# Three reorderings around tiles 3 to 8 of a fused linear-attention and SwiGLU kernel: one aggregation, two z sums, one clip and max-add

## The chip, the cores and the metric

The kernel runs on one core of a Trainium2 chip. The metric is the device time of one execution in microseconds (us). The engines are named as in the profile: PE is TensorE (PEld its weight loads), DVE is VectorE, ACT is ScalarE, POOL is GpSimd, SP is SyncE (SPq its queue of issued DMAs).

## What is computed

The input x has 2048 rows of 512 numbers. It is normalised row by row, and the result xn feeds a linear attention with 32 heads of 16 and a gated feed-forward block of width 1792. Both outputs are added to x.

```python
def _A_ref(x, wqkv, wo):                      # linear attention
    ...
    phi = lambda t: jnp.where(t > 0, t + 1, jnp.exp(t)) + 1e-6
    pq, pk = phi(q), phi(k)
    kv = jnp.einsum("bhsd,bhse->bhde", pk, v)
    z = jnp.einsum("bhsd->bhd", pk)
    num = jnp.einsum("bhqd,bhde->bhqe", pq, kv)
    den = jnp.einsum("bhqd,bhd->bhq", pq, z)[..., None] + 1e-6
    o = num / den
    return ... o ... @ wo

def _B_ref(x, w_gate, w_up, w_down):          # gated feed-forward
    return (_silu(x @ w_gate) * (x @ w_up)) @ w_down

xn = _layernorm(x, axis=-1)
return x + _A_ref(xn, A_wqkv, A_wo) + _B_ref(xn, B_w_gate, B_w_up, B_w_down)
```

## The kernel before

The 2048 rows are 16 tiles of 128 rows, and a tile is 128x512. The kernel has a front part, in which every tile is normalised, projected to keys and queries and accumulated, and a feed-forward part, in which TensorE runs the gate, up and down projections and the attention output for the rest of the span. The change touches the front part alone.

Every instruction is appended by hand to a list of its engine, in the order in which the calls stand in the program. An engine runs its list in order. `K.op` and `K.dma` take the names that an instruction reads (`r`) and writes (`w`), and put in front of it the semaphore waits that follow from earlier writers and readers. So the order of the calls sets the order on each engine, and a name in `r` that the instruction does not need for its data is a way to hold it back: it waits for the last writer of that name.

What happens to a tile t, with the lines at which its instructions appear in the profile:

- `bns(t)` (L297) and `agg(t)` (L300), on DVE: the row statistics, and mean and variance from them.
- `eps(t, "pool")` (L325) and `rstd_of(t)` (L334), on POOL: variance plus 1e-5, and its power of -0.5, both of one number per row. `stat(t)` is these four in a row.
- `xn(t)`: `xn_dve(t)` (L314), on DVE, normalises the tile, and `transpose_dma(t)` (L408), issued on SP, writes the transposed tile to `xnT`. Tile 3 is normalised by `xn_dve(3)` and transposed later.
- `kproj(t)` and `qproj(t)` (L417), on PE: four matmuls each, from `xnT` to a PSUM bank. Tiles 0 to 3 are projected before they are normalised (`proj_first`, L431) and scaled by `rstd` when the bank is read.
- `exp_k(t)` (L465), `exp_q(t)` (L471) and `copy_q(t)` (L477), on ACT: they read those banks. For the first tiles `first_ek` (L501) and `first_pk` (L507) do so, the latter into `kpos`.
- `clip_k(t)` (L484) and `maxadd_k(t)` (L493), on DVE: they turn the exponential and the bank into the key feature `pkq[:, t, 0, :]`. For tiles 1 to 3 `first_feat(t)` (L533) adds `kpos` and the clipped exponential instead, both in SBUF.
- `zsum(t, e)` (L557 for tile 0, L561 for the others), on POOL: adds the tile's key feature to `zacc`. Tile 0's is a cast, which starts the sum. The argument e names a buffer of exponentials whose last writer it waits for.
- `gtacc(t)` (L569), on PE: four matmuls that add the product of the normalised tile and its key feature to four PSUM banks. It needs `xn` and the key feature of the tile.

The order on PE around the change is `proj_first(3)`, `gtacc(1)`, `gtacc(2)`, `kproj(4)`, `qproj(4)`, `gtacc(3)`, `kproj(5)`, `qproj(5)`, `gtacc(4)`, `kproj(6)`, `qproj(6)`, `gtacc(5)` and so on. The order on POOL is `rstd(3)`, `rstd(5)`, `eps(6)`, `rstd(6)`, `zsum(0)`, `eps(7)`, `rstd(7)`, `eps(8)`, `rstd(8)`, `zsum(1)`, `eps(9)`, `rstd(9)`, `zsum(2)`. On DVE it is `xn(5)`, `bns(6)`, clip 3, `agg(6)`, `first_feat(3)`, `xn(6)`, `xn(3)`, `bns(7)`, `agg(7)`, `bns(8)`, `agg(8)`, clip 4, `xn(7)`, max-add 4, `bns(9)`, `agg(9)`, `xn(8)`, clip 5, max-add 5. SP issues the transpose of tile 6, the load of the input tiles 14 and 15, and the transposes of tiles 7, 8 and 9.

From tile 5 on a loop writes the steps of a tile: the two projections, the three ACT readings, the normalisations in `XN0[t]`, `feat_k(t)` (clip, then the z sum of tile t - 3, then max-add), and the statistics in `STAT[t]`.

Of the kernel before, what the change touches and what calls it, by code (L numbers as in the profile page):

```python
# [14 lines left out]
NT = S // P  # L15
# [93 lines left out]
def bass_parallel_sum__linear_attn_block__swiglu_ffn__prompt_kernel(  # L109
# [13 lines left out]
    pe, act, dve, pool, sp = nc.tensor, nc.scalar, nc.vector, nc.gpsimd, nc.sync  # L123
    bf, f32 = dt.bfloat16, dt.float32

    with contextlib.ExitStack() as es:
        E = es.enter_context

        def sb(name, shape, d=bf):
            return E(nc.sbuf_tensor(name, [P] + shape, d))  # L130
# [20 lines left out]
        NE = 3  # L151
        ek = sb("ek", [NE, D])
# [37 lines left out]
        def bk(i):  # L190
            return ("bank", i)
# [10 lines left out]
        def xload(eng, h, t0, n, after=()):  # L202
            K.dma(
                eng, lambda: h.dma_start(x_sb[:, t0:t0 + n, :], rows(xin, t0, n)),
                r=list(after), w=[("x", t0 + i) for i in range(n)],
            )
# [89 lines left out]
        def bns(t):  # L296
            K.op("dve", lambda: dve.bn_stats(stats[:, t, :], x_sb[:, t, :]), r=[("x", t)], w=[("st", t)])  # L297

        def agg(t):
            K.op("dve", lambda: dve.bn_aggr(mv[:, t, :], stats[:, t, :]), r=[("st", t)], w=[("mv", t)])  # L300
# [10 lines left out]
        def xn_dve(t):  # L311
            K.op(
                "dve",
                lambda: dve.tensor_scalar(  # L314
                    out=xn_sb[:, t, :], in0=x_sb[:, t, :], scalar1=mv[:, t, 0:1], scalar2=rstd[:, t:t + 1],
                    op0=ALU.subtract, op1=ALU.mult,
                ),
                r=[("x", t), ("mv", t), ("rstd", t)], w=[("xn", t)],
            )

        def eps(t, eng):
            h = dve if eng == "dve" else pool
            K.op(
                eng,
                lambda: h.tensor_scalar(  # L325
                    out=vpe[:, t:t + 1], in0=mv[:, t, 1:2], scalar1=1e-5, scalar2=None, op0=ALU.add,
                ),
                r=[("mv", t)], w=[("vpe", t)],
            )

        def rstd_of(t):
            K.op(
                "pool",
                lambda: pool.tensor_tensor(out=rstd[:, t:t + 1], in0=vpe[:, t:t + 1], in1=nhalf[:, :], op=ALU.pow),  # L334
                r=[("vpe", t), ("nhalf",)], w=[("rstd", t)],
            )
# [89 lines left out]
        def proj_first(t, wname, h):  # L426
            lo, b = (D, kb(t)) if wname == "wk" else (0, qb(t))
            K.op(
                "pe",
                [  # L430
                    (lambda c=c: pe.matmul(  # L431
                        banks[b], xcT[:, NDC * t + c, :], wqkv_sb[:, c, lo:lo + D],
                        start=(c == 0), stop=(c == NDC - 1),
                    ))
                    for c in (2 * h, 2 * h + 1)
                ],
                r=[("xcT", t, h)] + [(wname, i) for i in ((2, 3) if h else (0, 1))], w=[bk(b)],
            )
# [12 lines left out]
        def kb(t):  # L451
            return 2 * (t % 2)

        def qb(t):
            return 2 * (t % 2) + 1

        def kproj(t):
            proj(t, kb(t), D, "wk")

        def qproj(t):  # L460
            proj(t, qb(t), 0, "wq")
# [7 lines left out]
        def exp_q(t):  # L469
            K.op(  # L470
                "act", lambda: act.activation(eq[:, t, :], banks[qb(t)], ACT.Exp),  # L471
                r=[bk(qb(t))], w=[("eq", t)],
            )
# [16 lines left out]
        def maxadd(dst, src, e, r, w):  # L490
            K.op(
                "dve",
                lambda: dve.scalar_tensor_tensor(  # L493
                    out=dst, in0=src, scalar=0.0, in1=e, op0=ALU.max, op1=ALU.add,
                ),
                r=r, w=w,
            )
# [7 lines left out]
        def first_pk(t):  # L505
            K.op(
                "act", lambda: act.activation(kpos[:, t % NE, :], banks[kb(t)], ACT.Relu, scale=rstd[:, t:t + 1]),  # L507
                r=[bk(kb(t)), ("rstd", t)], w=[("kpos", t % NE)],
            )
# [7 lines left out]
        def first_pq(t):  # L517
            K.op(
                "act", lambda: act.activation(pkq[:, t, 1, :], banks[qb(t)], ACT.Identity, scale=rstd[:, t:t + 1]),
                r=[bk(qb(t)), ("rstd", t)], w=[("pq", t)],  # L520
            )
# [8 lines left out]
        def first_feat(t):  # L530
            K.op(
                "dve",
                lambda: dve.tensor_tensor(out=pkq[:, t, 0, :], in0=kpos[:, t % NE, :], in1=ek[:, t % NE, :], op=ALU.add),  # L533
                r=[("kpos", t % NE), ("ek", t % NE)], w=[("pk", t)],
            )

        def clip_k(t):
            clip(ek[:, t % NE, :], ("ek", t % NE))

        def maxadd_k(t):  # L540
            e = t % NE
            maxadd(pkq[:, t, 0, :], banks[kb(t)], ek[:, e, :], [bk(kb(t)), ("ek", e)], [("pk", t)])

        def feat_k(t):
            clip_k(t)
            zsum(t - 3, t % NE)
            maxadd_k(t)

        def feat_q(t):
            clip(eq[:, t, :], ("eq", t))  # L550
            maxadd(pkq[:, t, 1, :], pkq[:, t, 1, :], eq[:, t, :], [("eq", t), ("pq", t)], [("pq", t)])

        def zsum(t, e):
            pk = pkq[:, t, 0, :]
            after = [] if e is None else [("ek", e)]
            if t == 0:
                K.op("pool", lambda: pool.tensor_copy(zacc[:, :], pk), r=[("pk", t)] + after, w=[("zacc",)])  # L557
            else:
                K.op(
                    "pool",  # L560
                    lambda: pool.tensor_tensor(out=zacc[:, :], in0=zacc[:, :], in1=pk, op=ALU.add),  # L561
                    r=[("pk", t), ("zacc",)] + after, w=[("zacc",)],
                )

        def gtacc(t):
            K.op(
                "pe",
                [
                    (lambda c=c: pe.matmul(  # L569
                        banks[4 + c], xn_sb[:, t, c * P:(c + 1) * P], pkq[:, t, 0, :],  # L570
                        start=(t == 0), stop=(t == NT - 1),
                    ))
                    for c in range(NDC)
                ],
                r=[("xn", t), ("pk", t)], w=[bk(4 + c) for c in range(NDC)],
            )

        def stat(t):
            bns(t)
            agg(t)  # L580
            eps(t, "pool")
            rstd_of(t)

        def xn(t):
            xn_dve(t)
            if t >= 3:
                transpose_dma(t)
# [92 lines left out]
        rstd_of(5)  # L680
        xn(5)
        bns(6)
        first_pq(2)
        proj_first(3, "wk", 1)
        first_ek(3)
        clip_k(3)
        first_pk(3)
        agg(6)
        eps(6, "pool")
        rstd_of(6)  # L690
        zsum(0, 0)
        first_feat(3)
        gtacc(1)
        gtacc(2)
        xn(6)
        xload("sp", sp, 14, 2)
        xn_dve(3)
        bns(7)
        kproj(4)
        agg(7)  # L700
# [2 lines left out]
        exp_k(4)  # L703
        first_pq(3)
        qproj(4)
        stat(8)
        exp_q(4)
        copy_q(4)
        clip_k(4)
        zsum(1, 1)  # L710
        xn(7)
        maxadd_k(4)
        bns(9)
        agg(9)
        eps(9, "pool")
# [7 lines left out]
        for t in range(5, NT):  # L723
            kproj(t)
            exp_k(t)
            qproj(t)
            exp_q(t)
            copy_q(t)
            for i in XN0.get(t, ()):
                xn(i)  # L730
            feat_k(t)
            for i in STAT.get(t, ()):
                stat(i)
            for i in XN.get(t, ()):
                xn(i)
            if t in (6, 7, 8, 9):
                transpose_dma((3, 0, 1, 2)[t - 6])
            if t == 10:
                whalf("wg", wg_sb, B_w_gate, 0)
                whalf("wu", wu_sb, B_w_up, 0)  # L740
                wqkv_load("sp", sp, "wv", 2, 0, 4)
                wload("sp", sp, "wo", wo_sb, A_wo)
                whalf("wg", wg_sb, B_w_gate, 1)
            if t in (11, 12, 13, 14):
                late_eq(t - 11)
            if t == 12:
                masks()
            if t >= 12:
                gtacc(t - 2)
            elif t < 11:  # L750
                gtacc(t - 1)
        zsum(NT - 3, None)
        zsum(NT - 2, None)
        zsum(NT - 1, None)
        gtacc(NT - 2)
        gtacc(NT - 1)

# [292 lines left out]
```

## Time and profile before

| what | value |
|---|---|
| median of three runs | 212.15 us (211.47 to 212.44) |
| the profiled execution, its own time | 211.49 us |
| its span in the profile | 210.3 us |
| granted TensorE clock | 1.00 in every stage |
| busy: PE, DVE, ACT, POOL | 206.9, 119.8, 70.9, 74.1 us |
| busy between 15 and 20 us: PE, DVE, POOL | 4.75, 4.33, 3.45 us of 5.00 |
| busy between 20 and 25 us: PE, DVE, POOL | 5.00, 4.83, 4.83 us of 5.00 |
| bn_stats (L297), 128x512 | 679 ns mean |
| z sum (L561), 128x512 | 1156 ns mean |
| transpose of a tile by DMA, issue to landing | 2.5 us median, 4.1 us at most |

The span is the time between the first and the last instruction that the profile shows; the time of an execution has some overhead around it. An engine that is busy for 5.00 of 5.00 us in a stage has no idle time there, though matmuls overlap and their ends are modelled. The share of an engine over the whole span says little about the first 25 us, where DVE and POOL are close to full, and a good deal less busy later.

### The profile page before, as it was taken

Reading aid. Unit: us, or ns where it says so; the run is one execution under the profiler, and the core shown is the slowest. Engines: PE = TensorE matmul, PEld = TensorE weight load, DVE = VectorE, ACT = ScalarE, POOL = GpSimd, SP = SyncE. Lnnn points to the kernel's source line nnn. Section 1 sums busy time; section 2 is a strip of 40 time slices with the busy share of each in tenths; the row PEclk is TensorE's granted clock in tenths of the full one; section 3 lists DMA queues with packets and bytes.
Section 4 is the critical chain, followed back from the end, with each engine's and each line's share of the span. In section 5 each row is a group of like instructions: output and inputs, shape, how many; then the busy total and the mean of one; then the engine's idle time right before and its main releaser. Section 6 shows DMA issues by size and latency. Waiting matters only on the chain.

```text
span 210.3 us, 2774 instructions
## 1 busy us (share of the span) xinstructions
PE 206.9 (98%) x987; PEld 94.6 (45%) x987; DVE 119.8 (57%) x246; ACT 70.9 (34%) x125; POOL 74.1 (35%) x95
## 2 busy tenths in 40 slices
PE   7999999999999999999999999999999999999996
PEld 2443444445444444444444444444444444444444
DVE  3989989335365774547365746365556535374122
ACT  5877666966643331303122312213032213121000
POOL 3647987658032444222140432230414032221200
DMA  6774444795792011110202110202021010310201
GB/s 201 221 198 95 86 100 100 215 371 183 199 357 58 3 29 27 41 25 28 51 0 50 25 28 25 50 0 50 3 50 25 27 25 25 44 37 25 50 25 53
DMA packets 30287, 16.84 MB, mean 80 GB/s; under 512 B 20928, under 2 KB 29632, under 8 KB 30272
## 3 DMA queue, kind: packets, MB, share of 16 engines
q1 hardware_dynamic: 29984, 16.39, 29.4%
q10 hardware_dynamic: 288, 0.26, 0.4%
q8 instruction: 8, 0.13, 0.2%
q14 instruction: 7, 0.06, 0.1%
HBM read 9.70 MB, written 2.10 MB: 56 GB/s over the span
## 4 chain that ended last, share of the span: by engine, by line
PE 90%; DVE 4%; POOL 3%; issue 1%; DMA 1%; ACT 0%; DVEq 0%
PE psum L770 46%; PE psum L953 23%; PE psum L417 8%; PE psum L942 7%; PE psum L569 5%; POOL rstd L334 1%; DVE stats L297 1%; DMA x_sb<-in_A_x_dram 1%; DVE xn_sb L314 1%; DVE pkq L533 1%; POOL vpe L325 1%; POOL pkq L526 1%; DVE mv L300 0%; PE psum L868 0%; PE psum L891 0%
## 5 line engine op out<-in xcount | busy, mean ns | idle before, releaser
L785 ACT ACTIVATE sg<-psum 128x512 bf16<-128x512 f32 x56 | 33.4, 598 | 106.8 <-PE psum L770 106.0
L770 PE MATMUL psum<-xnT,wu_sb 128*128 128x512 bf16 x224 | 57.5, 379 | 0.0
L770 PE MATMUL psum<-xnT,wg_sb 128*128 128x512 bf16 x224 | 57.5, 379 | 0.0
L900 POOL TENSOR_TENSOR prod<-pkq,zb 128x512 f32<-128x512 bf16 x16 | 18.6, 1161 | 57.8 <-DVE pkq L493 57.8
L770 PEld LDWEIGHTS psum<-xnT,wu_sb 128*128 128x128 bf16 x224 | 21.9, 98 | 26.4
L770 PEld LDWEIGHTS psum<-xnT,wg_sb 128*128 128x128 bf16 x224 | 21.9, 98 | 26.2
L966 DVE TENSOR_TENSOR out_sb<-psum,x_sb 128x512 bf16<-128x512 f32 (+2 forms) x17 | 11.2, 660 | 35.9 <-PE psum L953 35.9
L924 POOL TENSOR_TENSOR pqn<-pkq,rden 128x512 bf16<-128x512 bf16 x16 | 16.9, 1057 | 36.6 <-DVE rden L918 36.6
L791 DVE TENSOR_TENSOR pkq<-psum,sg 128x512 bf16<-128x512 f32 x28 | 19.1, 687 | 18.5 <-PE psum L770 14.1
L791 DVE TENSOR_TENSOR xn_sb<-psum,sg 128x512 bf16<-128x512 f32 x28 | 18.8, 673 | 14.1 <-PE psum L770 13.6
L953 PE MATMUL psum<-wd_sb,xn_sb 128*128 128x512 bf16 (+2 forms) x126 | 25.7, 355 | 0.0
L953 PE MATMUL psum<-wd_sb,pkq 128*128 128x512 bf16 x112 | 25.5, 379 | 0.0
L417 PE MATMUL psum<-wqkv_sb,xnT 128*128 128x512 bf16 x96 | 22.5, 379 | 0.0
L561 POOL TENSOR_TENSOR zacc<-zacc,pkq 128x512 f32<-128x512 f32 x15 | 17.3, 1156 | 4.9 <-DVE ek L484 4.6
L953 PEld LDWEIGHTS psum<-wd_sb,xn_sb 128*128 128x128 bf16 x126 | 11.8, 98 | 12.5
L953 PEld LDWEIGHTS psum<-wd_sb,pkq 128*128 128x128 bf16 x112 | 11.0, 98 | 13.2
L942 PE MATMUL psum<-m_sb,eq 128*128 128x512 bf16 (+2 forms) x68 | 16.6, 366 | 0.0
L569 PE MATMUL psum<-pkq,xn_sb 128*128 128x512 bf16 x64 | 16.0, 379 | 0.3
L417 PEld LDWEIGHTS psum<-wqkv_sb,xnT 128*128 128x128 bf16 x96 | 9.3, 98 | 11.5 <-DMA xnT<-xn_sb 0.4
L908 DVE TENSOR_REDUCE den<-prod 128x32 f32<-128x512 f32 x16 | 10.9, 684 | 5.7 <-POOL prod L900 5.7
L297 DVE BATCH_NORM_STATS2 stats<-x_sb 128x6 f32<-128x512 bf16 x16 | 10.9, 679 | 3.3 <-DMA x_sb<-in_A_x_dram 3.2
L493 DVE SCALAR_TENSOR_TENSOR pkq<-pkq,eq 128x512 bf16<-128x512 bf16 x16 | 11.1, 692 | 0.6
(65 smaller groups left out, 140.6 us busy)
## 6 DMA issues: line engine op xcount, KB each, us to landing
out_dram<-out_sb SPq DMA_DIRECT2D x15, 128.0 KB, 1.7
wg_sb<-in_B_w_gate_dram SPq DMA_DIRECT2D x2, 896.0 KB, 7.9
wu_sb<-in_B_w_up_dram SPq DMA_DIRECT2D x2, 896.0 KB, 6.0
wd_sb<-in_B_w_down_dram SPq DMA_DIRECT2D x1, 1792.0 KB, 9.8
x_sb<-in_A_x_dram SPq DMA_DIRECT2D x5, 256.0 KB, 3.4
x_sb<-in_A_x_dram SPq DMA_DIRECT2D x5, 128.0 KB, 3.5
wqkv_sb<-in_A_wqkv_dram SPq DMA_DIRECT2D x5, 128.0 KB, 3.7
wqkv_sb<-in_A_wqkv_dram SPq DMA_DIRECT2D x1, 512.0 KB, 7.9
```

Source lines behind the costliest of these rows:

```text
L297: K.op("dve", lambda: dve.bn_stats(stats[:, t, :], x_sb[:, t, :]), r=[("x", t)], w=[("st", t)])
L417: (lambda c=c: pe.matmul(banks[b], xnT[:, c, t * P:(t + 1) * P], wqkv_sb[:, c, lo:lo + D], start=(c == 0), stop=(c == NDC - 1),))
L561: lambda: pool.tensor_tensor(out=zacc[:, :], in0=zacc[:, :], in1=pk, op=ALU.add),
L569: (lambda c=c: pe.matmul(banks[4 + c], xn_sb[:, t, c * P:(c + 1) * P], pkq[:, t, 0, :], start=(t == 0), stop=(t == NT - 1),))
L770: (lambda c=c: pe.matmul(banks[b], w_sb[:, c, fc * P:(fc + 1) * P], xnT[:, c, C * 512:(C + 1) * 512], start=(c == 0), stop=(c == NDC - 1),))
L785: lambda: act.activation(sg[:, j % NSG, :], banks[gb], ACT.Silu),
L791: lambda: dve.tensor_tensor(out=hT(C, fc), in0=banks[ub], in1=sg[:, j % NSG, :], op=ALU.mult,),
L900: lambda: pool.tensor_tensor(out=p, in0=pkq[:, t, 1, :], in1=zb[:, :], op=ALU.mult),
L924: lambda: pool.tensor_tensor(out=pqn[:, t % NPN, :].rearrange("p (h e) -> p h e", e=DH), in0=pkq[:, t, 1, :].rearrange("p (h e) -> p h e", ...
L942: (lambda g=g: pe.matmul(dst, pqnT(t)[:, g, :], m_sb[:, g, lo:hi], start=(g == 0), stop=False,))
L953: (lambda fc=fc: pe.matmul(dst, hT(C, fc)[:, jj * P:(jj + 1) * P], wd_sb[:, fc, lo:hi], start=False, stop=(fc == NFC - 1),))
L966: lambda: dve.tensor_tensor(out=o, in0=src, in1=x_sb[:, t, lo:hi], op=ALU.add),
```

## The change

Three things move, and no instruction is added or removed:

1. `agg(6)`, `eps(6)` and `rstd_of(6)` are called right behind `bns(6)`. On DVE `agg(6)` comes ahead of clip 3; on POOL the order of these calls stays.
2. `zsum` takes a list of names to wait for. `zsum(0)` is called behind `xn_dve(3)` and waits for the normalised tile 3, not for clip 3. `zsum(1)` is called behind `xn(7)` and waits for the normalised tile 7, not for clip 4. On POOL `zsum(1)` now stands ahead of `eps(8)` and `rstd(8)`.
3. Clip 4 and max-add 4 come ahead of `xn(7)`, and `xn(7)` ahead of the statistics of tile 8.

The order on DVE is then `xn(5)`, `bns(6)`, `agg(6)`, clip 3, `first_feat(3)`, `xn(6)`, `xn(3)`, `bns(7)`, `agg(7)`, clip 4, max-add 4, `xn(7)`, `bns(8)`, `agg(8)`, `bns(9)`, `agg(9)`, `xn(8)`, clip 5, max-add 5. The order on POOL is `eps(6)`, `rstd(6)`, `zsum(0)`, `eps(7)`, `rstd(7)`, `zsum(1)`, `eps(8)`, `rstd(8)`, `eps(9)`, `rstd(9)`, `zsum(2)`.

```diff
         def feat_k(t):
             clip_k(t)
-            zsum(t - 3, t % NE)
+            zsum(t - 3, [("ek", t % NE)])
             maxadd_k(t)
...
-        def zsum(t, e):
+        def zsum(t, after=()):
             pk = pkq[:, t, 0, :]
-            after = [] if e is None else [("ek", e)]
+            after = list(after)
...
         rstd_of(5)
         xn(5)
         bns(6)
+        agg(6)
+        eps(6, "pool")
+        rstd_of(6)
         first_pq(2)
         proj_first(3, "wk", 1)
         first_ek(3)
         clip_k(3)
         first_pk(3)
-        agg(6)
-        eps(6, "pool")
-        rstd_of(6)
-        zsum(0, 0)
         first_feat(3)
         gtacc(1)
         gtacc(2)
         xn(6)
         xload("sp", sp, 14, 2)
         xn_dve(3)
+        zsum(0, [("xn", 3)])
         bns(7)
         kproj(4)
         agg(7)
...
         qproj(4)
-        stat(8)
         exp_q(4)
         copy_q(4)
         clip_k(4)
-        zsum(1, 1)
+        maxadd_k(4)
         xn(7)
-        maxadd_k(4)
+        zsum(1, [("xn", 7)])
+        stat(8)
         bns(9)
         agg(9)
         eps(9, "pool")
...
-        zsum(NT - 3, None)
-        zsum(NT - 2, None)
-        zsum(NT - 1, None)
+        zsum(NT - 3)
+        zsum(NT - 2)
+        zsum(NT - 1)
```

## The prediction

> **What bounds the kernel now.** I read the page first: the busy tenths of the span and the chain that ended last. Then I read that chain in order of time, and last the timeline from 12.3 to 21.2 us, where the edited lines run.
>
> The page (40 slices of 5.26 us):
>
> ```profile
> PE   7999999999999999999999999999999999999996
> DVE  3989989335365774547365746365556535374122
> ```
>
> TensorE is full from the second slice on, so an edit in the first 23 us can pay only by the gaps that TensorE still has there. The chain in order of time (start, length, what) shows where they end:
>
> ```profile
> 18.86 0.29 issue
> 19.15 0.70 DVE pkq L493
> 19.85 0.05 issue
> 19.89 1.04 PE psum L569 x4
> 20.93 1.79 PE psum L417 x8
> 22.72 0.86 PE psum L569 x4
> 23.59 1.73 PE psum L417 x8
> ```
>
> From 22.72 us the chain is TensorE alone, to the last output. Four 128x512 matmuls issue in 0.86 us and eight in 1.73. The timeline (start, length, engine; in brackets the idle time before, and its releaser) shows the gaps and the rows that I cost with:
>
> ```profile
> 12.42 0.65 POOL L334 TENSOR_TENSOR rstd<-vpe,nhalf 128x1 f32<-128x1 f32 x1 [1.17 <-DVE vpe L325]
> 12.58 0.68 DVE L533 TENSOR_TENSOR pkq<-kpos,ek 128x512 bf16<-128x512 f32 x1
> ...
> 14.81 0.69 DVE L533 TENSOR_TENSOR pkq<-kpos,ek 128x512 bf16<-128x512 f32 x1 [0.20 <-ACT kpos L507]
> 15.01 0.92 POOL L334 TENSOR_TENSOR rstd<-vpe,nhalf 128x1 f32<-128x1 f32 x1
> 15.89 0.61 POOL L557 CAST zacc<-pkq 128x512 f32<-128x512 bf16 x1
> ...
> 17.02 0.55 PEld L569 LDWEIGHTS psum<-pkq,xn_sb 128*128 128x128 bf16 x4 [0.64 <-DVE xn_sb L314]
> ...
> 19.63 1.16 POOL L561 TENSOR_TENSOR zacc<-zacc,pkq 128x512 f32<-128x512 f32 x1
> 19.89 0.55 PEld L569 LDWEIGHTS psum<-pkq,xn_sb 128*128 128x128 bf16 x4 [0.60 <-DVE pkq L493]
> 20.82 0.33 PEld L417 LDWEIGHTS psum<-wqkv_sb,xnT 128*128 128x128 bf16 x3 [0.39 <-DMA xnT<-xn_sb]
> ```
>
> Three waits are left. gtacc(3) starts at 17.02, when xn(3) is done; kproj(4) and qproj(4) had the array until 14.98 + 1.73 = 16.71, so 0.31 us are lost. gtacc(4) starts at 19.89, when max-add 4 is done; the array was free at 17.89 + 1.73 = 19.62: 0.27. kproj(6) starts at 20.82, when the transposed tile 6 lands; free at 19.89 + 0.86 = 20.75: 0.07. Together 0.65 us, 0.31% of the span. That caps the gain. A loss has no such cap. What counts is when gtacc(5) starts, at 22.56 now: behind it nothing is late.
>
> **The change, part by part.** Nothing is added or removed; TensorE, ScalarE and SyncE keep their order. Only VectorE and POOL are reordered, and zsum(0) and zsum(1) wait for xn(3) and xn(7) instead of clip 3 and clip 4.
>
> *Aggregation 6 ahead of clip 3.* bn_stats 6 starts at 13.50, and an aggregation follows 0.71 after its statistics (16.89 to 17.60), so agg(6) starts at 14.21, not 14.44. Clip 3 moves from 14.23 to 14.31 (0.10 per aggregation) and ends at 14.60. First_feat(3) waits for kpos until 14.78 anyway, which hides that; without that cover it would cost 0.08. POOL: agg ends 14.39, eps(6) 0.08 later for 0.22, rstd(6) from about 14.78. Does rstd(6) then end early? The rows speak against it: the 128x1 power takes 0.57 to 0.63 alone, but 0.92 at 15.01, beside first_feat(3), which reads two SBUF tensors: it ended 0.43 after that instruction. First_feat(3) still starts at 14.81, so I let rstd(6) be held again and end at 15.93. The bounds are 15.35 (14.78 + 0.57) and 15.93; I take 15.93, the row of the same pair of instructions. The move is worth nothing.
>
> [...]
>
> *zsum(0) held for xn(3).* The cast ran from 15.89 to 16.50, and xn(6), from 16.03, took 0.60 beside it; xn(8) at 20.57 took 0.38 alone. With the cast behind xn(3): xn(6) 16.03 to 16.41, xn(3) 16.35 to 16.75 (next start after 0.32), gtacc(3) at 16.81 (0.06 later, as before). The gap shrinks from 0.31 to 0.10. The transpose of tile 6 is issued 0.22 earlier on SyncE's queue, at 16.45 instead of 16.67; with its 4.1 us to landing it is there at 20.56. The cast now runs 16.83 to 17.44; VectorE then has bn_stats 7, and a z sum beside bn_stats 9 (19.63 and 19.75) slowed nothing. Queued behind the waiting cast is only eps(7), not due before 17.65.
>
> *Clip and max-add 4 ahead of statistics 8.* VectorE: bn_stats 7 16.68, agg(7) 17.39 to 17.57, clip 4 17.49 (its exponential ended at 16.71), max-add 4 17.81 to 18.50. gtacc(4) is due at 16.81 + 0.86 + 1.73 = 19.40 and starts then: its 0.27 is gone. kproj(6), due at 20.26, waits for its transpose until about 20.6; then gtacc(5) is due at 20.6 + 1.73 = 22.33.
>
> *What is late next.* Before, rstd(8) was ready at 19.66, before zsum(1) began. Now the order on POOL is eps(7), rstd(7), zsum(1), eps(8), rstd(8), and zsum(1) waits for xn(7). eps(7) starts at 17.65 beside clip 4 and ends at 17.87 to 17.99 (the eps at 20.76, begun inside xn(8), took 0.43 instead of 0.22); rstd(7) ends at 18.53 to 18.65; xn(7) starts 0.10 later and ends at 19.01 to 19.13 (before: 19.23). From there, in order: signal 0.08, zsum(1) 1.16, eps(8) 0.22 starting 0.03 before the sum's end, 0.09, rstd(8) 0.57, signal 0.10, then start to start xn(8) 0.30 and clip 5 0.32, max-add 5 0.69, signal 0.06: 3.56 us. VectorE's own queue (statistics 8 and 9, ending near 20.8) hides none of the wait for rstd(8); it stands idle about half a microsecond, where before it ran xn(8) at 20.57. So gtacc(5) starts at 22.57 to 22.69 against 22.56.
>
> *Sum.* Recovered 0.21 at gtacc(3) and 0.27 at gtacc(4); given back about 0.3 at kproj(6), and 0.24 to 0.36 at gtacc(5): +0.01 to +0.13, middle +0.07 us. Behind gtacc(5) VectorE has a 2.16 us period (max-adds at 21.19, 23.35, 25.51) against TensorE's 2.59, so max-add 6 ends near 24.7 for a gtacc(6) due at 25.2, and the room grows by 0.43 a tile. The profiled execution took 211.49 us around its span of 210.3, so it would become 211.56; the median of the three runs is 212.15 (211.47 to 212.44), 0.66 above it, and I put the same +0.07 there: 212.2. [...]
>
> **Rivals.**
> 1. *rstd(6) gets through before first_feat(3)*, because the race is decided within 0.03 us (14.78 against 14.81). With eps(6) slowed by clip 3 and the power ending at 15.50, xn(6) starts at 15.60, agg(7) at 16.96, xn(7) ends at 18.70, and gtacc(5) starts at 18.70 + 3.56 = 22.26: 0.3 gained. With neither held it is 0.5. For: the early aggregation. Against: the 0.92 row. Time 211.75.
> 2. *Slower: zsum(2) falls on xn(9).* rstd(8) is late, so all of POOL is, and zsum(2) comes after rstd(9): at 22.1, or 22.5 if eps(9) is held by xn(8). xn(9) starts at 23.37. A normalisation that began at 34.15, just behind a sum at 34.08, took 1.23 instead of 0.38: 0.85 lost. Of that 0.43 is covered by the room at gtacc(6), so the total is +0.07 + 0.42, about 212.6. It decides if zsum(2) starts after about 22.9, since earlier ones let go in time. Repeated at xn(10) and xn(11), each adding 0.42 (0.85 less the 0.43 of room gained a tile), it reaches +1.3. For: POOL is full and late. Against: my start is 0.4 too early for it.
> 3. *The power holds first_feat(3)*: begun at 14.78, it keeps the 14.81 instruction waiting until 15.35. First_feat(3) then ends at 16.04 and lets xn(6) start 0.60 after its own start, at 15.95 instead of 16.03: 0.08 off everything, 212.15. For: the power would be first by 0.03. Against: first_feat(2), begun inside a power, took 0.68.
>
> **How the numbers follow.** Forecast 0.62; rival 1 0.17; rival 2 0.15, over half of it repeated; rival 3 0.06. The range goes from the 0.5 of rival 1, and the scatter of the runs below their median, to the single collision of rival 2 plus the 0.3 of scatter above: 211.4 to 212.9. About 0.5% (1.06 us) is what a measurement of this kernel can tell from no change. Faster by that is out of reach of the 0.65 us of gaps, so 0.03 is left for what I have misread. Slower takes the repeated collision and a little for a wait that I have not seen: 0.10. Same: 0.87.
>
> **What would show it.** Right: rstd(6) still about 1 us long and ending near 15.9; xn(6) 0.38; TensorE's wait for L493 at gtacc(4) gone; VectorE idle before xn(8) with L334 as releaser; a new TensorE wait of 0.2 to 0.4 for L493 at gtacc(5), near 22.6. Wrong: a power of 0.57 ending by 15.5 (rival 1); a 128x512 normalisation of 0.8 us or more between 23 and 28 us, with a TensorE wait for L493 after 25 us (rival 2); first_feat(3) starting or ending 0.5 later (rival 3); gtacc(5) at 22.3 or earlier with no wait before it, by which the price of the held sum would be refuted.

## The result, and the profile after

| | median | lowest to highest |
|---|---|---|
| before, 22 runs | 211.94 us | 211.32 to 212.44 |
| changed kernel, 22 runs | 211.23 us | 210.81 to 212.10 |

The ratio is 0.9975, with a 95% interval of 0.9965 to 0.9984: the change takes 0.5 us off (0.34 to 0.74). A second comparison of the same kernel gave 0.9979 (0.9963 to 0.9994). The forecast was +0.07 us, so it had the wrong sign. 211.23 also lies below the range, which began at 211.4.

The profiled execution of the changed kernel took 212.10 us, the slowest of its 22, with a span of 210.9. So its rows can't be laid beside those of before by their clock times. The page (40 slices):

```profile
PE   8999999999999999999999999999999999999996
DVE  4888899434364775546274746364556535374122
```

TensorE is fuller than before in the first slice, but with slow matmuls. Its first eight took 3.57 us and the twelve of L444 took 3.48; in before they took 3.26 and 2.76. TensorE went from 0.43 us to 0.216 us a matmul at 6.9 us here and near 4 us there, and bn_stats 6 starts at 14.22 instead of 13.50. Each kernel scatters by over 1 us in its times, and where bn_stats 6 starts is part of that scatter: every profile of this study that has the original front took 188.92 to 188.95 us from the start of gtacc(5) to the end of its time. What the change is worth is therefore best read from the distance between the start of bn_stats 6 and the start of gtacc(5): 9.06 us in before (13.50 to 22.56) and 8.95 here (14.22 to 23.17). The two rows of before:

```profile
13.50 0.68 DVE L297 BATCH_NORM_STATS2 stats<-x_sb 128x6 f32<-128x512 bf16 x1
...
22.56 1.03 PE L569 MATMUL psum<-pkq,xn_sb 128*128 128x512 bf16 x4
```

The chain of the changed kernel in order of time (start, length, what):

```profile
15.53 1.13 POOL rstd L334
16.66 0.03 issue
16.69 0.73 DVE xn_sb L314 x2
...
19.24 0.42 DVE xn_sb L314
19.67 0.07 issue
19.74 1.16 POOL zacc L561
20.89 0.20 POOL vpe L325
21.09 0.07 issue
21.16 0.58 POOL rstd L334
21.75 0.03 issue
21.77 0.03 DVE xn_sb L314
...
22.42 0.70 DVE pkq L493
23.12 0.05 issue
23.17 1.04 PE psum L569 x4
```

This is the chain of the prediction link by link: the power of tile 6, the two normalisations, xn(7), z sum 1, eps and power of tile 8, xn(8), clip and max-add 5, gtacc(5). The timeline has the waits that go with it:

```profile
14.22 0.69 DVE L297 BATCH_NORM_STATS2 stats<-x_sb 128x6 f32<-128x512 bf16 x1
...
15.53 1.12 POOL L334 TENSOR_TENSOR rstd<-vpe,nhalf 128x1 f32<-128x1 f32 x1
15.53 0.69 DVE L533 TENSOR_TENSOR pkq<-kpos,ek 128x512 bf16<-128x512 f32 x1 [0.22 <-ACT kpos L507]
16.69 0.73 DVE L314 TENSOR_SCALAR xn_sb<-x_sb,mv,rstd 128x512 bf16<-128x512 bf16 x2 [0.46 <-POOL rstd L334]
17.48 0.55 PEld L569 LDWEIGHTS psum<-pkq,xn_sb 128*128 128x128 bf16 x4 [0.37 <-DVE xn_sb L314]
21.13 1.41 PEld L417 LDWEIGHTS psum<-wqkv_sb,xnT 128*128 128x128 bf16 x8 [0.52 <-DMA xnT<-xn_sb]
21.77 0.41 DVE L314 TENSOR_SCALAR xn_sb<-x_sb,mv,rstd 128x512 bf16<-128x512 bf16 x1 [0.50 <-POOL rstd L334]
23.16 0.33 PEld L569 LDWEIGHTS psum<-pkq,xn_sb 128*128 128x128 bf16 x3 [0.62 <-DVE pkq L493]
```

The power is held for 1.12 us, the two normalisations take 0.73 together (0.93 in before), the wait at gtacc(4) is gone, VectorE idles 0.50 us before xn(8), and gtacc(5) waits for max-add 5. Here the prediction looks right in every row. But these rows give 0.11 us, and the runs say 0.5.

The two rows at 15.53 hold the question: the power and first_feat(3) start in the same hundredth of a microsecond. Two theories follow. **A**: this is rival 1. In most executions the power wins the tie; the profiled ones happen to show it losing. **B**: the power is held in all executions, and the gain comes from the front or from elsewhere.

### The profile page after: what moved, and what is told of

It is laid out like the page before. It is cut to its first block, busy times and chain, and to the rows that moved or that the text cites. A ratio compares the mean times of both kernels' runs of the same rounds, so it can differ in the third digit from the quotient of the medians.

```text
span 210.9 us, 2773 instructions
## 1 busy us (share of the span) xinstructions
PE 208.0 (99%) x987; PEld 95.3 (45%) x987; DVE 119.5 (57%) x246; ACT 70.9 (34%) x125; POOL 74.3 (35%) x95
## 4 chain that ended last, share of the span: by engine, by line
PE 92%; DVE 3%; POOL 2%; ACT 1%; issue 1%
PE psum L770 46%; PE psum L953 23%; PE psum L417 7%; PE psum L942 7%; PE psum L569 5%; PE psum L444 2%; PE psum L269 2%; POOL rstd L334 1%; DVE xn_sb L314 1%; DVE pkq L533 1%; ACT pkq L519 1%; DVE stats L297 1%; PE psum L389 1%; POOL zacc L561 1%; PE psum L868 0%
```

## The experiments

### One step undone, one step changed, one step alone

Four kernels, timed side by side with before. The first is the changed kernel again.

> The changed kernel, profiled once more. In its first profile TensorE's cold matmuls (0.43 us each) went on until 6.9 us, in that of before only until about 4 us, so the two front parts are shifted by 0.7 us. Theory A (rival 1: the power of tile 6 gets ahead of first_feat(3) where TensorE is fast early): in an execution with the step near 4 us, the L334 row near 14.8 us is 0.57 to 0.65 long, gtacc(5) starts at 22.0 to 22.3 and the time is near 210.9. Theory B (the power is held there too, and the gain comes from the other executions): the row is 0.9 to 1.1 long, gtacc(5) starts at 22.5 to 22.7 and the time is near 211.5. Median by both 211.2.

It took 211.46 us (median of 12; 210.81 to 212.13). Its profiled execution took 211.53 with the power at 1.12 and gtacc(5) 8.93 us behind bn_stats 6: the held case again.

```diff
@@ agg6_back, against the changed kernel
         bns(6)
-        agg(6)
-        eps(6, "pool")
-        rstd_of(6)
...
         clip_k(3)
         first_pk(3)
+        agg(6)
+        eps(6, "pool")
+        rstd_of(6)
         first_feat(3)
```

> The changed kernel with the aggregation, eps and power of tile 6 back behind clip 3. Theory A: the gain hangs on the early power, so the time goes back to 211.8 to 212.0. Theory B: the move is worth nothing, the time stays at 211.2 to 211.3.

211.67 us, ratio to before 1.0001 (0.9988 to 1.0014): against before the whole gain is gone, as A says. Against the changed kernel beside it, it is slower by 0.2 us in the medians, 0.35 in the means and 0.5 by the two ratios, so the size is less clear than the direction; and its profile (distance 9.01) differs from the held profiles of the changed kernel by 0.06 to 0.08 us only.

```diff
@@ z1_behind_stat8, against the changed kernel
         xn(7)
-        zsum(1, [("xn", 7)])
         stat(8)
+        zsum(1, [("xn", 7)])
```

> The changed kernel with zsum(1) behind the statistics of tile 8 on POOL, so that the power of tile 8 doesn't wait for it. If the held z sum is what makes gtacc(5) late, as the prediction's sum has it (xn(8) idle 0.5 us, then 0.24 to 0.36 us at gtacc(5)): 0.25 to 0.35 us faster than the changed kernel, 210.9, no idle time before xn(8), and gtacc(5) straight behind the eight matmuls of tile 6. If gtacc(5) is not what is late, 211.2 as the changed kernel.

211.96 us, ratio to before 1.0001 (0.9987 to 1.0015). That was a miss: 0.5 us slower than the changed kernel, where 0.3 faster was expected. Its profiled distance is 9.34 us, 0.4 more than in the profiles of the changed kernel. Two rows of its timeline and the wait that follows show why:

```profile
21.20 1.15 POOL L561 TENSOR_TENSOR zacc<-zacc,pkq 128x512 f32<-128x512 f32 x1
21.27 1.23 DVE L314 TENSOR_SCALAR xn_sb<-x_sb,mv,rstd 128x512 bf16<-128x512 bf16 x1 [0.21 <-POOL rstd L334]
...
23.48 0.55 PEld L569 LDWEIGHTS psum<-pkq,xn_sb 128*128 128x128 bf16 x4 [0.92 <-DVE pkq L493]
```

With the z sum behind the power, both it and xn(8) are released by that power. The sum starts 0.07 us ahead, and xn(8) takes 1.23 us instead of 0.41. This is the collision of rival 2, one tile earlier than feared, and in a kernel that tried to avoid the idle time. The idle 0.50 us before xn(8) in the changed kernel is the cheaper of the two.

The same profile shows a second thing, ahead of bn_stats 6 and so outside the distance:

```profile
12.52 1.25 POOL L334 TENSOR_TENSOR rstd<-vpe,nhalf 128x1 f32<-128x1 f32 x1 [0.97 <-DVE vpe L325]
12.68 0.69 DVE L533 TENSOR_TENSOR pkq<-kpos,ek 128x512 bf16<-128x512 f32 x1
```

These are the power of tile 5 and first_feat(2). In the other nineteen profiles of this study the power, begun at the same place (0.16 us into xn(2) and 0.16 ahead of first_feat(2)), took 0.65 us. Here it took 1.25, and bn_stats 6 started 3.42 us behind gtacc(0) instead of 2.83 or 2.84. So there is another race, one tile earlier and in every version, worth 0.6 us; how often it is lost in the runs that were not profiled isn't shown.

```diff
@@ maxadd4_only, against before
         qproj(4)
-        stat(8)
         exp_q(4)
         copy_q(4)
         clip_k(4)
-        zsum(1, 1)
-        xn(7)
         maxadd_k(4)
+        xn(7)
+        stat(8)
+        zsum(1, 1)
```

> The kernel before with clip and max-add 4 ahead of tile 7's normalisation and tile 8's statistics, everything else as before (zsum(1) stays behind rstd(8) on POOL). By the prediction's sum the 0.27 us at gtacc(4) is recovered and given back at kproj(6), whose transposed tile lands at 20.8 as before: 0.07 to 0.1 us faster at most, 211.85. If the landing of that tile doesn't bind, 0.25 to 0.3 us faster, 211.65.

212.59 us, ratio 1.0034 (1.0020 to 1.0048): another miss, since 0.07 to 0.3 us faster was expected, and the third part of the change alone makes the kernel slower by 0.7 us. The wait at gtacc(4) is gone, but statistics 8 come later, and the same collision appears:

```profile
21.52 1.16 POOL L561 TENSOR_TENSOR zacc<-zacc,pkq 128x512 f32<-128x512 f32 x1
21.59 1.24 DVE L314 TENSOR_SCALAR xn_sb<-x_sb,mv,rstd 128x512 bf16<-128x512 bf16 x1 [0.20 <-POOL rstd L334]
...
23.80 0.54 PEld L569 LDWEIGHTS psum<-pkq,xn_sb 128*128 128x128 bf16 x4 [1.06 <-DVE pkq L493]
```

So holding z sum 1 behind xn(7), ahead of eps 8, is what keeps the third part from doing harm.

### More profiles, and the power put ahead

> The changed kernel, one more profile. In both of its profiles so far the power of tile 6 was held by first_feat(3) (1.12 us), both at 211.5 us or more, and gtacc(5) started 8.93 to 8.95 us behind the start of bn_stats 6, against 9.06 in the profile of before: that explains 0.12 of the measured 0.5 us. Every profile so far took 188.94 us from the start of gtacc(5) to the end of its time. Theory A: an execution of the changed kernel near 210.9 us has the power at 0.57 to 0.65 and gtacc(5) 8.4 to 8.6 us behind bn_stats 6. Theory B: it is 8.95 in all of them, and an execution near 210.9 has bn_stats 6 starting near 13.0.

> As the run before it: the changed kernel, one more profile. Theory A: 8.4 to 8.6 us from bn_stats 6 to gtacc(5) where the time is near 210.9. Theory B: 8.95 always.

> The kernel before, one more profile. Theory A: 9.06 us from the start of bn_stats 6 to gtacc(5) as in its first profile, whatever the start of the front. Theory C: the first profile of before was a lucky one, and the usual distance is 9.3 to 9.5 with the same times from bn_stats 6 on in the changed kernel.

The two profiles of the changed kernel took 211.46 and 211.55 us, both with the power at 1.12 us and a distance of 8.93 and 8.94. The new profile of before took 212.16 us with a distance of 9.23 (14.00 to 23.23). Its kproj(6) waited longer for the transposed tile than in the first profile:

```profile
21.49 1.41 PEld L417 LDWEIGHTS psum<-wqkv_sb,xnT 128*128 128x128 bf16 x8 [0.56 <-DMA xnT<-xn_sb]
```

So before's distance changes with the landing of tile 6, while the changed kernel, when held, follows max-add 5. 9.23 lies between theory A's 9.06 and theory C's 9.3 to 9.5. By these distances the held case gains 0.1 to 0.3 us, not 0.5.

```diff
@@ eps6_dve, against the changed kernel
         agg(6)
-        eps(6, "pool")
+        eps(6, "dve")
         rstd_of(6)
```

> The changed kernel with eps(6) on VectorE right behind its aggregation, so that the power of tile 6 starts about 0.25 us sooner, ahead of first_feat(3). Theory A and the prediction's rival 1: the power takes 0.57 to 0.65, xn(6) starts when first_feat(3) lets go, and the time is 0.2 to 0.4 us below the changed kernel in all executions, median 210.9 to 211.1. Theory B (the front decides, the power is not what is late): 211.2 to 211.4.

211.17 us, ratio to before 0.9977 (0.9966 to 0.9989), between A's 210.9 to 211.1 and B's 211.2 to 211.4. In its timeline the power comes first:

```profile
14.81 0.55 POOL L334 TENSOR_TENSOR rstd<-vpe,nhalf 128x1 f32<-128x1 f32 x1 [1.61 <-DVE vpe L325]
15.03 0.69 DVE L533 TENSOR_TENSOR pkq<-kpos,ek 128x512 bf16<-128x512 f32 x1
15.64 0.73 DVE L314 TENSOR_SCALAR xn_sb<-x_sb,mv,rstd 128x512 bf16<-128x512 bf16 x2
```

xn(6) follows first_feat(3) at once, and gtacc(5) starts 8.48 us behind bn_stats 6. By its profile it should beat the held kernel by 0.45 us, yet it timed only 0.1 to 0.2 below the changed kernel (mean 211.25 against 211.36 over the 36 runs of that kernel so far). That speaks for A, but the scatter is too large to settle it.

### A steady front

If the scatter comes from the start, the start can be fixed. The first try put 12 multiplications on a scratch tile ahead of bn_stats 0 and ran 26 warming matmuls:

```diff
-        fill(8, 512)
+        fill(26, 512)
+        K.op("dve", lambda: dve.memset(prod[:, :, :], 0.0), ...)
+        for _ in range(12):
+            K.op("dve", lambda: dve.tensor_scalar(out=prod[:, :, :], in0=prod[:, :, :], scalar1=1.0, ...), ...)
         bns(0)
```

> The kernel before with a steady front: VectorE runs a memset and 12 multiplications by one on a scratch tile ahead of the first bn_stats (some 7 us), and TensorE runs 26 warming matmuls in place of 8, so that its step to full speed and the first loads lie behind it whatever the execution. The front starts later by 5 to 6 us; what matters is the difference to the other three of this call, which have the same front. Both theories: the distance from bn_stats 6 to gtacc(5) is 9.06 to 9.23 us as in the two profiles of before, and the runs scatter by 0.3 us instead of 1.2.

> The changed kernel with the same steady front (extra VectorE work and warming matmuls). In four profiles of it the power of tile 6 and first_feat(3) started at the same hundredth of a microsecond, and the power was held. Theory A (in executions without the profiler the power often wins that tie): 0.4 to 0.6 us below w_before and near w_eps6_dve. Theory B (always held): 0.1 to 0.3 below w_before, as the distances 8.95 against 9.06 and 9.23 say, and 0.4 to 0.5 above w_eps6_dve.

> The changed kernel with the aggregation of tile 6 back behind clip 3, and the steady front. There the power starts 0.2 us behind first_feat(3), so there is no tie. Theory A: 0.3 to 0.5 us above w_after. Theory B: 0.06 above w_after (distance 9.01 against 8.95).

> The changed kernel with eps(6) on VectorE, and the steady front. There the power starts 0.2 us ahead of first_feat(3) and takes 0.55; distance 8.48. Theory A: within 0.2 us of w_after. Theory B: 0.4 to 0.5 us below w_after. Both: 0.5 to 0.75 us below w_before.

The medians were 221.41, 220.40, 220.57 and 219.86 us, with up to 2.7 us between the runs of one kernel: useless for half a microsecond. The multiplications took 8.7 us, TensorE was idle for 2.3 to 3.6 us behind its warming matmuls, and in three of the four profiles its granted clock then fell (its mean over the span is 0.992 in w_before and w_agg6_back, 0.985 in w_after, 1.00 in w_eps6_dve). The row of the page of w_after, 5.5 us a slice:

```profile
PEclk9958999999999999999999999999999999999999
```

The second try had 7 multiplications and 21 matmuls, after which the array pauses for at most 1.4 us in the four profiles.

> The kernel before with the front steadied in a second way: 7 scratch multiplications on VectorE (0.73 us each) and 21 warming matmuls, so that the array waits at most 1.3 us between the last of them and the first tile (in the version before this one it waited up to 3.6 us and was slow again afterwards). The first bn_stats comes at about 7.1 us, some 4 us later than in before. Only differences within this call count. Distance from bn_stats 6 to gtacc(5) 8.99 to 9.23 us, scatter of the runs below 0.5 us.

> The changed kernel with that steadied front. Theory A (without the profiler the power of tile 6 often wins its tie with first_feat(3)): 0.4 to 0.6 us below v_before, 0.3 to 0.45 below v_agg6_back, within 0.2 of v_eps6_dve, though the profiled execution may show the power held. Theory B (held in all executions): 0.06 to 0.3 below v_before, 0.07 below v_agg6_back, 0.45 above v_eps6_dve.

> The changed kernel with the aggregation of tile 6 back behind clip 3, steadied front: no tie, the power is held. Theory A: 0.3 to 0.45 us above v_after. Theory B: 0.07 above v_after. Both: 0 to 0.2 below v_before.

> The changed kernel with eps(6) on VectorE, steadied front: no tie, the power is ahead. Theory A: within 0.2 us of v_after. Theory B: 0.45 below v_after. Both: 0.5 to 0.75 below v_before.

| | median | lowest to highest | distance, profiled |
|---|---|---|---|
| v_before | 215.26 | 215.21 to 215.51 | 9.28 |
| v_agg6_back | 215.31 | 215.23 to 215.33 | 9.08 |
| v_after | 214.65 | 214.63 to 214.73 | 8.51 |
| v_eps6_dve | 214.72 | 214.71 to 214.73 | 8.47 |

The scatter is down to 0.1 us, 0.3 in v_before, and the four fall into two pairs 0.6 us apart. With this front theory A holds: the changed kernel times like the version with the power ahead, and with the aggregation put back it times like before. The difference between v_after and v_agg6_back, 0.66 us, is above the 0.3 to 0.45 that A forecast. And the profile of v_after shows the tie won:

```profile
18.59 0.57 POOL L334 TENSOR_TENSOR rstd<-vpe,nhalf 128x1 f32<-128x1 f32 x1
18.60 0.72 DVE L533 TENSOR_TENSOR pkq<-kpos,ek 128x512 bf16<-128x512 f32 x1 [0.23 <-ACT kpos L507]
```

One hundredth of a microsecond earlier than first_feat(3), the power takes 0.57 us; in the same hundredth, it took 1.12.

### The first part alone

What is left is whether the other two parts have any share. Before with the three lines of tile 6 moved and nothing else (the diff of agg6_back, the other way round, with zsum(0) left behind clip 3), in both fronts:

> The kernel before with the first part of the change alone (aggregation, eps and power of tile 6 ahead of clip 3), steadied front. Theory A1 (the early power is the whole gain, the other two parts only move stalls about): max-add 4 ends near 23.0 us, just in time for gtacc(4) at 23.1, xn(8) keeps its place and gtacc(5) starts at 25.7 to 25.8: 214.6 to 214.75, as v_after. Theory A2 (the parts need one another): the cast of z sum 0 follows the early power and meets xn(6), as it did before, max-add 4 is late again for gtacc(4), and the time lies between v_after and v_before, 214.9 to 215.2.

> The same one part on the kernel before, with its own front. Theory A1: 0.4 to 0.6 us below the kernel before, 211.2 to 211.4, as the changed kernel. Theory A2: 0.1 to 0.3 below, 211.5 to 211.75.

v_agg6_only took 214.73 us (214.72 to 215.00), distance 8.50: the whole gain. agg6_only took 211.08 us (210.95 to 212.36), ratio 0.9986; its interval, 0.9969 to 1.0003, doesn't exclude 1, since five of its twelve runs were above 211.6; whether those lost a race isn't shown. Its timeline, with its own front, has the tie won too:

```profile
14.94 0.57 POOL L334 TENSOR_TENSOR rstd<-vpe,nhalf 128x1 f32<-128x1 f32 x1
14.95 0.72 DVE L533 TENSOR_TENSOR pkq<-kpos,ek 128x512 bf16<-128x512 f32 x1 [0.23 <-ACT kpos L507]
...
15.46 0.68 POOL L557 CAST zacc<-pkq 128x512 f32<-128x512 bf16 x1
15.59 1.02 DVE L314 TENSOR_SCALAR xn_sb<-x_sb,mv,rstd 128x512 bf16<-128x512 bf16 x2
...
19.53 0.55 PEld L569 LDWEIGHTS psum<-pkq,xn_sb 128*128 128x128 bf16 x4 [0.42 <-DVE pkq L493]
```

The cast of z sum 0 still meets xn(6) (1.02 for the two normalisations instead of 0.73), and gtacc(4) still waits for max-add 4: it starts at 19.54, where the array is free at 16.85 + 0.86 + 1.73 = 19.44. That is 0.1 us of the former 0.27, and it is all that is left: gtacc(5), at 22.14, follows straight on, and the distance is 8.50. With the power early everything is early enough, and the second and third part have nothing to add. Without the first part they have nothing to give either: v_agg6_back timed 0.05 us above v_before, where 0 to 0.2 below was expected. No version beat the changed kernel by more than the runs can tell.

## Why the prediction was wrong, point by point

**The step that failed** is the first term of the sum: "I take 15.93, the row of the same pair of instructions. The move is worth nothing." The two bounds, 15.35 and 15.93, were right, and so was the start (1.28 us behind bn_stats 6; measured 1.31), but the row that I took was of a power that started 0.20 us behind first_feat(3). For a tie it decided nothing. With the steady front the power ends 1.87 us behind the start of bn_stats 6 instead of 2.43, and the move is worth 0.6 us. That is rival 1, with its reason (a race within 0.03 us) and its size (0.3 to 0.5); it had 0.17. The slow eps(6) that it allowed for didn't come (0.22 us in after, v_after and agg6_only).

How often the changed kernel wins the tie with its original front isn't shown directly. The fastest of the 109 runs of before took 211.28 us. A held execution of the changed kernel has a distance 0.13 shorter than the first profile of before (8.93 against 9.06), so that for a time under about 211.15 it would need an earlier start than any of those runs had; 11 of the 36 runs lie below. By this estimate these at least won the tie. If the held executions time like agg6_back (mean 211.79) and the others like eps6_dve (211.25), the mean of 211.36 makes it about four in five, but with twelve runs in each of the two anything from a half to all fits. Why its four profiles with the original front, and that of w_after, all show the tie lost stays open.

**The rest of the chain was right where the power is held.** The forecast of +0.07 us fits the versions that hold it for certain: agg6_back timed 1.0001 of before (0.9988 to 1.0014), v_agg6_back 0.05 us above v_before. From bn_stats 6, forecast and profile of the changed kernel: gtacc(3) 3.31 and 3.26; gtacc(4) 5.90 and 5.86; kproj(6) 7.1 and 6.92; the end of xn(7) 5.51 to 5.63 and 5.43; from there to gtacc(5) 3.56 and 3.52. The 0.50 us before xn(8) and the new wait at gtacc(5) are in the profile. The sum came out 0.12 to 0.24 us too late at gtacc(5), half of the upper figure because eps(7) was not held by clip 4 (0.22 at 18.33). Its listed terms also don't add to its total: 0.21 and 0.27 recovered against 0.3 and 0.24 to 0.36 given back is +0.06 to +0.18. The stated +0.01 to +0.13 is the difference of the two starts of gtacc(5).

**The baseline was one profile**, but a usable one. Before's distance was 9.06 and 9.23, 8.99 in w_before, where the tile had landed in time, and 9.28 in v_before. The last belongs to the slowest run of v_before (215.51). If bn_stats 6 starts at 17.30 in its other three runs too, as it does within 0.01 us in all five profiles with that front, their 215.21 to 215.26 mean a distance of 8.98 to 9.03.

**The range** began at 211.4. Rival 1's full 0.5 below the median of three runs is 211.65, and those runs reach 0.68 below their median; I allowed 0.25 of it. The larger sample of before also has its median 0.2 lower. And about 0.5% was too coarse for what can be told apart: with these numbers of runs the intervals reach 0.1 to 0.2% to each side.

**Rival 2** did not come in the changed kernel, but its mechanism and price were right: 1.23 and 1.24 us in two variants, against the 1.23 that it was priced from.

**Rival 3**, the power holding first_feat(3) to its end, is refuted: in v_after first_feat(3) began 0.01 us into the power and took 0.72, 0.03 longer than the 0.69 of before. In these profiles the one that began in the same hundredth or second took longer: the power of tile 6, up to 0.20 us behind first_feat(3), 0.92 to 1.12, ending 0.42 or 0.43 after it (the powers of tiles 7 to 9 in before took 0.57 to 0.63), and xn(8), 0.07 behind z sum 1 in z1_behind_stat8 and maxadd4_only, 1.23 and 1.24, ending 0.15 after it (0.38 in before).

## What to carry to other kernels

When a forecast rests on who comes first, and the two are within a few hundredths of a microsecond, no row of a clear order prices it: keep both cases whole, and move the instruction by a few tenths more to see what each is worth. When every execution starts differently, measure distances from a fixed instruction inside the trace, and steady the start before asking for half a microsecond. A fixed instruction hides what happens ahead of it, so compare the rows before it as well: that is where the race of tile 5 stood. A change of several parts should be run part by part: here one part had the gain, another alone lost 0.7 us, and a third paid for that.

## What the runs showed of the hardware

Beside an addition with two SBUF inputs (first_feat(3), 0.69 us), the power of one number per row took 0.55 us when it began 0.22 us ahead (eps6_dve) and 0.57 when 0.01 ahead (v_after, agg6_only). It took 1.12 when it began in the same hundredth (after), 1.00 when 0.11 behind (z1_behind_stat8) and 0.92 when 0.20 behind (before); in these three it ended 0.42 or 0.43 us after the addition. The addition lost at most 0.03 us. Beginning first is not always enough: the power of tile 5, begun inside a normalisation and 0.16 us ahead of first_feat(2), took 0.65 in nineteen profiles and 1.25 in one, where it ended 0.40 us after first_feat(2).

TensorE's first matmuls took 0.43 us each until about 4 us (before) and 6.9 us (after) into the span, and 128x512 ones 0.216 from there on, though the granted clock reads 1.00 in both profiles throughout. In the profiles with 26 warming matmuls the granted clock fell later in the span behind an idle time of 2.79 us (w_before, mean of the span 0.992), 2.88 (w_agg6_back, 0.992) and 3.58 (w_after, 0.985, with 5 tenths in the third slice of its page); behind 2.34 us (w_eps6_dve) it stayed at 1.00.
